# Two layers of cached attention and an MLP, decoded on one core: V rows placed by K chunk, and the softmax joins asked for an item later

## The chip, the cores and the metric

The kernel runs on one core of a Trainium2 chip. The core has five engines that run side by side, each with its own queue of instructions in a fixed order: TensorE (PE in the profile; PEld is its weight loading), VectorE (DVE), ScalarE (ACT), GpSimd (POOL) and SyncE (SP). Here SP only issues DMA transfers. The transfers are carried out by 16 DMA engines, which move data from the memory of the chip to the core's on-chip memory of 128 partitions. The metric is device microseconds for one execution. The kernel before takes 1147.62 us, the median of three runs from 1143.37 to 1153.54.

## The reference

Two blocks, A and B, are applied in turn, twice each. B's mixing part works on a sequence of one token, so that its shifted slices are all zero; what is left of it is a layer norm and an MLP. A is attention of one new token per row of the batch over a cache of keys and values. The batch has 8 rows; there are 16 query heads and 8 cache heads, 4096 cached positions and a head size of 256; the model width is 448.

```python
def _A_ref(x, k_cache, v_cache, wq, wo):
    q = (x @ wq).reshape(B, Sq, Hq, Dh)          # 8 x 1 x 16 x 256
    k = jnp.repeat(k_cache, rep, axis=1)         # two query heads share one cache head
    v = jnp.repeat(v_cache, rep, axis=1)
    scores = einsum(q, k) * (Dh ** -0.5)
    p = softmax(scores)
    return einsum(p, v).reshape(B, Sq, Hq * Dh) @ wo

x = A_x
x = x + _A_ref(_layernorm(x), A_k_cache, A_v_cache, A_wq, A_wo)
x = x + _B_ref(_layernorm(x), B_w1, B_w2, B_w3, B_w4)
x = x + _A_ref(_layernorm(x), A_k_cache, A_v_cache, A_wq, A_wo)
x = x + _B_ref(_layernorm(x), B_w1, B_w2, B_w3, B_w4)
```

Each pass over the attention reads both caches, 134 MB each, less what the kernel keeps on the chip from the first pass.

## The kernel before, in words

**Units, chunks, items.** One unit is one row of the batch and one pair of cache heads (`gp`, four pairs), in one of the two passes (`ps`). A unit's keys are cut into four chunks of 1 MB and its values too. An item is one chunk of K (`kv` 0), one chunk of V (`kv` 1) or one block of weights (`kv` 2). The order of the items is planned in Python before anything is issued (`block`, `first_kept`, `weights`), and one long loop over `items` (L1335) emits the instructions of each. The engines then run what was emitted in that order; an instruction waits for the semaphores of what it needs, and what stands behind it in its queue waits with it.

**Reads.** `emit_loads` (L972) walks the same list of items ahead of the work. It takes a free place of 8 KB on each partition (17 places, `places`) for each chunk and issues the read on SP: K by `load_k` (L949), V by `load_v` (L958; whole chunks at L967, halves at L970), weights by `load_weights` (L1017) and `load_tail` (L1011). SP stops at a read whose place is still in use. In `load_k` partition p takes consecutive rows of K from a region of 32 KB of its own. In `load_v` partition p takes 16 consecutive rows of V, 8 KB, and the 128 partitions of one chunk follow each other in memory.

**K items.** The chunk is transposed in blocks by VectorE (`transpose_k`, L1036); TensorE forms the scores of two chunks in `sc` (`scores`, L1051). After every second chunk the list `exps_due` is given an entry, and `flush` at the next item calls `exps` (L1059): VectorE takes the maximum over each partition's scores (as the minimum of the negated scores, L1061) and ScalarE writes the exponentials to `p_n` (L1062). A maximum is thus known for each partition and each half `u` of the chunks. With the second half comes the join: TensorE brings the two halves' maxima to all partitions (L1073, two matmuls of float32), ScalarE and VectorE choose between them with the mask `which` (even or odd pairs of partitions hold one half or the other, L1080 and L1087), VectorE finds the least (L1081) and subtracts it (L1091), and ScalarE takes the exponential (L1094). The result, `down`, corrects each partition's p to a common maximum.

**V items.** `turn_p` transposes p by TensorE (L1135) and VectorE scales it with `down` (L1142). `sum_p` sums p over the positions by TensorE (L549), and VectorE reduces and inverts the sums (L553, L559). `spread_p` copies p into the layout that the V products need (L1329), and `pv` multiplies p by V (L1154). All these small results share one bank, `misc`, so the next matmul into it has to wait until the last one was read.

**Between items** `step` advances generators that carry the rest of the layer: normalisation of the outputs (`half`, L589), the output projection, the MLP (`mlp`, with w3 by `wblk` at L503 and w4 at L463) and the next pass's query projection. Some of the V chunks stay on the chip for the second pass; `away` (L1116) and `back` (L1121) move parts of them.

Of the kernel before, what the change touches and what calls it, by code (L numbers as in the profile page):

```python
# [17 lines left out]
def kernel(  # L18
# [36 lines left out]
    assert D == 448 and F % 256 == 0  # L55
# [55 lines left out]
    def small(n):  # L111
# [5 lines left out]
    which = small(2)  # L117
    nc.vector.tensor_reduce(
        which,
        ident.rearrange("p (i u x) -> p u i x", u=2, x=2),  # L120
        mybir.AxisListType.XY,
        ALU.add,
    )
# [130 lines left out]


# [241 lines left out]
    def mlp_hidden(b0, nb):  # L497
# [3 lines left out]
        for c in range(HC):  # L501
            for fc in range(4):
                w, xi = wblk(w3_sb, F, c, fc)  # L503
                if nb == 1:
                    wide(h_ps[:, c : c + 1], w, xbs(1)[:, xi, :], fc == 0, fc == 3)
                    continue
                nc.tensor.matmul(
                    h_ps[:, c * nb : c * nb + nb],
                    w,
                    xbs(nb)[:, xi, :],  # L510
                    start=(fc == 0),
                    stop=(fc == 3),
                )
# [31 lines left out]
    def sum_p(who, p_of_unit):  # L545

        z_ps = misc[:, 0:32]
        for t in range(4):
# [3 lines left out]
        rz_of[who] = rz_free.pop(0)  # L552
        nc.vector.tensor_reduce(  # L553
            rz_t[:, rz_of[who]],
            z_ps.rearrange("p (n m) -> p n m", n=4),
            mybir.AxisListType.X,
            ALU.add,
        )
        nc.vector.reciprocal(rz_t[:, rz_of[who]], rz_t[:, rz_of[who]])  # L559
# [29 lines left out]
    def half(rec, ps, b, gps, OT, ready, tight=False):  # L589
# [8 lines left out]
        for k, gp in enumerate(gps):  # L598
            while (ps, b, gp) not in rz_of:
                yield  # L600
# [138 lines left out]
    q_rows = {4: (0, 0, 4), 5: (1, 0, 5), 7: (0, 4, 7)}  # L739
    q_final = [(1, 5, 8), (0, 7, 8)]  # L740
# [92 lines left out]
    for gp in free:  # L833
        weights("q", (gp, 0, Bn))
# [123 lines left out]
    def load_v(it, dst):  # L958
# [3 lines left out]
        src = rows.rearrange("(a p y) d -> a p (y d)", a=4, y=16)[it[2]]  # L962
        if halfway(it):
            nc.sync.dma_start(dst[:, 0 : PR * Dh], src[:, 0 : PR * Dh])
            nc.sync.dma_start(rest_t[:], src[:, PR * Dh :])
        elif loads and it not in halved:
            nc.sync.dma_start(dst, src)  # L967
        else:
            for y0, y1 in ((0, 8), (8, 16)) if loads else ((0, 8), (8, 12), (12, 16)):
                nc.sync.dma_start(dst[:, Dh * y0 : Dh * y1], src[:, Dh * y0 : Dh * y1])  # L970

    def emit_loads(most=None):  # L972
        n = 0
        while loads and places and n != most:
# [21 lines left out]
            if not open_:  # L996
                break
            p = pick(open_)
            taken(it, p)
            n += 1  # L1000
            if kv == 2:
                load_weights(slots[p], tasks[k][2], tasks[k][1])
# [14 lines left out]
    def load_weights(dst, kind, rows):  # L1017

        if kind == "o":
# [5 lines left out]
        src = A_wq[:, HU * rows[0] : HU * rows[0] + HU]  # L1025
        nc.sync.dma_start(
            dst[:, 0 : 3 * HU].rearrange("p (f c) -> p f c", f=3),
            src[0:384].rearrange("(f p) c -> p f c", f=3),
        )
        load_tail(dst[:, 3 * HU : 3 * HU + HU // 2], src)  # L1030
# [28 lines left out]
    def exps(p_sb, u):  # L1059
# [3 lines left out]
            p_sb[:, :, :, 2 * u : 2 * u + 2].rearrange("p t i x -> p x t i"),  # L1063
# [5 lines left out]
        if u == 0:  # L1069
            return  # L1070
        both = misc[:, 0:64]
        for k in range(2):
            nc.tensor.matmul(  # L1073
                both[:, 32 * k : 32 * k + 32],
                low_max[:, k : k + 1].to_broadcast([128, 128]),
                lanes[:],
                start=True,
                stop=True,
            )
        nc.scalar.mul(down, both[:, 0:32], which[:, 0:1])  # L1080
        nc.vector.tensor_reduce(  # L1081
            least,
            both.rearrange("p (u n m) -> p n u m", u=2, n=4),
            mybir.AxisListType.XY,
            ALU.min,
        )
        nc.vector.scalar_tensor_tensor(  # L1087
            down, both[:, 32:64], which[:, 1:2], down, ALU.mult, ALU.add
        )
        by_head = down.rearrange("p (n m) -> p n m", n=4)  # L1090
        nc.vector.tensor_tensor(  # L1091
            by_head, by_head, least.unsqueeze(2).to_broadcast([128, 4, 8]), ALU.subtract
        )
        nc.scalar.activation(down, down, ACT.Exp, scale=-1.0)  # L1094

    exps_due = []

    def flush():
        while exps_due:
            exps(*exps_due.pop(0))  # L1100
# [30 lines left out]
    def transpose_p(p_sb, p_to):  # L1131

        pt_ps = misc[:, 0:128].rearrange("p (t m) -> p t m", t=4)
        for t in range(4):
            nc.tensor.matmul(  # L1135
                pt_ps[:, t],
                p_sb[:, t].rearrange("p i x -> p (i x)"),
# [4 lines left out]
        nc.vector.tensor_tensor(  # L1142
            p_to, pt_ps, down.unsqueeze(1).to_broadcast([128, 4, 32]), ALU.mult
# [48 lines left out]
    emit_loads(2)  # L1192
# [28 lines left out]
    nc.sync.dma_start(w4_sb[:], B_w4.rearrange("(c p) d -> p c d", p=128))  # L1221
# [98 lines left out]
    def turn_p():  # L1320
        n = next(iter(p_of))
        slot_of[n] = free_slots.pop(0)
        transpose_p(p_of.pop(n), psv[slot_of[n]])

    def spread_p(it):
        if it in ring_of or it in plain or it[0] not in slot_of:
            return
        ring_of[it] = v_items.index(it) % 2
# [4 lines left out]
    kept_q = items[12]  # L1333

    for idx, it in enumerate(items):  # L1335
# [26 lines left out]
        if kv:  # L1362
            flush()
        if kv == 2:
# [8 lines left out]
            else:  # L1373
                gp_q, r0, r1 = rows
                nb = r1 - r0

                def q_of_block(c, fc, qw=slot):
                    if fc < 3:
                        return qw[:, fc * HU + 128 * c : fc * HU + 128 * c + 128], fc
                    k = 2 * 128 * c // HU  # L1380
                    at = 3 * HU + 128 * c - k * HU // 2
                    return qw[:, at : at + 128], 3 + k

                ps_q = (
                    store[0][:, 256 : 256 + 8 * nb] if nb == Bn else misc[:, 192 : 192 + 8 * nb]
                )
# [316 lines left out]
```

## Time and profile before

| what | value |
|---|---|
| median of the three runs | 1147.62 us |
| the profiled execution, its own time | 1153.23 us |
| its span from first to last instruction | 1151.1 us |
| mean granted clock of TensorE | 0.591 |
| TensorE busy | 732.3 us (64%) |
| weight loads busy | 472.2 us (41%) |
| VectorE busy | 654.0 us (57%) |
| ScalarE busy | 263.8 us (23%) |
| bytes read | 419.63 MB, 365 GB/s over the span |

The span is the profiled execution from its first instruction to its last; 2.1 us of the execution lie outside it. The chain that ended last is followed back from the last instruction to what released it, again and again; its shares tell what the time was spent waiting for. The costliest lines by busy time are the K transposes on VectorE (L1036, 445.7 us in 384 instructions), the scores on TensorE (L1051, 246.0 us) and the V products (L1154, 239.1 us). ScalarE's exponentials (L1062) take 105.9 us in 128 instructions, and the float32 matmuls of the joins (L1073) 74.2 us.

### The profile page before, as it was taken

To read this page: it belongs to the slowest core of one execution; us is meant where nothing else is said; L and a number is where in the kernel's file an instruction comes from. 1 tells how busy PE (TensorE), PEld (TensorE's weight loads), DVE (VectorE), ACT (ScalarE), POOL (GpSimd) and SP (SyncE) were. 2 spreads that over 40 slices of the span, in tenths; PEclk is the share of its full clock that TensorE was granted. 3 is DMA by queue.
4 is the path that set the end of the run, shared out by engine and by line. 5 is a ranking of instruction groups with operands and counts; after the bars stand their busy time and mean duration, and the time that the engine had idled before them with its cause. 6 is when DMAs were issued, how large, how long until landed. Compare 5 with 4: busy or idle time off the path is not lost.

```text
span 1151.1 us, 29813 instructions
## 1 busy us (share of the span) xinstructions
PE 732.3 (64%) x13109; PEld 472.2 (41%) x13109; DVE 654.0 (57%) x1388; ACT 263.8 (23%) x808; POOL 16.3 (1%) x27
## 2 busy tenths in 40 slices
PE   3255557665676667666775677557665775567776
PEld 2133334443354344433442345334433543345455
DVE  6255684188417851686258724782388237842764
ACT  1021111231124111422132114211421142112311
POOL 0000000000000000000000000000000000000000
PEclk9955555665655555556656575556655665575555
DMA  9999999988899779889989799987988998969994
GB/s 381 393 422 422 420 422 358 418 368 327 329 414 423 305 263 408 363 329 341 392 336 424 296 371 420 395 311 293 408 355 326 369 418 356 416 247 415 378 424 192
DMA packets 69297, 421.57 MB, mean 366 GB/s; under 512 B 7080, under 2 KB 12976, under 8 KB 43568
## 3 DMA queue, kind: packets, MB, share of 16 engines
q1 hardware_dynamic: 69120, 419.66, 90.8%
q8 instruction: 103, 1.69, 0.6%
q14 instruction: 26, 0.21, 0.0%
q10 hardware_dynamic: 48, 0.01, 0.0%
HBM read 419.63 MB, written 0.01 MB: 365 GB/s over the span
## 4 chain that ended last, share of the span: by engine, by line
DVE 36%; PE 27%; DMA 24%; ACT 6%; issue 4%; SPq 2%; POOL 0%; DVEq 0%; ACTq 0%
DVE places L1036 26%; DMA places<-in_A_v_cache_dram 16%; PE sc L1051 12%; DMA places<-in_A_k_cache_dram 9%; PE o L1154 6%; ACT p_n L1062 4%; DVE few L1061 3%; PE misc L210 2%; PE misc L625 2%; DVE store L1116 2%; DVE few L1081 1%; ACT down L1080 1%; SPq L967 1%; SPq L229 1%; DVE down L1087 1%
## 5 line engine op out<-in xcount | busy, mean ns | idle before, releaser
L1036 DVE STREAM_TRANSPOSE places<-places 128x512 uint32<-128x512 uint32 (+2 forms) x384 | 445.7, 1212 | 17.8 <-DMA places<-in_A_k_cache_dram 15.0
L1051 PE MATMUL sc<-places,qbd 128*8 128x256 bf16 (+1 forms) x4736 | 246.0, 362 | 191.3 <-DVE places L1036 174.3
L1154 PE MATMUL o<-places,ptw 128*8 128x256 bf16 x3808 | 239.1, 386 | 113.4 <-DMA places<-in_A_v_cache_dram 83.9
L1051 PEld LDWEIGHTS <-qbd 128*8 128x8 bf16 x4736 | 128.0, 106 | 263.8 <-issue 111.7
L1062 ACT ACTIVATE p_n<-sc,few 128x256 bf16<-128x256 f32 x128 | 105.9, 827 | 498.4 <-DVE few L1061 409.2
L1154 PEld LDWEIGHTS <-ptw 128*8 128x8 bf16 x3968 | 101.3, 104 | 174.7 <-issue 93.6
L1061 DVE TENSOR_REDUCE few<-sc 128x1 f32<-128x256 f32 x128 | 53.0, 414 | 96.2 <-PE sc L1051 80.1
L1073 PE MATMUL misc<-lanes,few 128*128 128x32 f32 x256 | 74.2, 393 | 30.4 <-DVE few L1061 17.1
L1329 ACT COPY ptw<-psv 128x32 bf16<-128x32 bf16 x248 | 54.0, 233 | 160.2 <-PE o L1154 151.3
L1073 PEld LDWEIGHTS misc<-lanes,few 128*128 128x128 f32 x256 | 59.3, 296 | 56.6 <-DVE few L1061 24.6
L625 PE MATMUL misc<-R_t,o_t 128*128 128x4 f32 (+1 forms) x212 | 48.7, 336 | 23.5 <-DVE R_t L601 9.6
L625 PEld LDWEIGHTS misc<-R_t,o_t 128*128 128x128 f32 x212 | 44.3, 290 | 40.5 <-ACT o_t L580 16.4
L1081 DVE TENSOR_REDUCE few<-misc 128x4 f32<-128x64 f32 x64 | 14.3, 224 | 71.6 <-ACT down L1080 71.6
L448 ACT CAST qbd<-misc 32x16 bf16<-32x16 f32 (+1 forms) x184 | 31.1, 169 | 53.9 <-PE misc L442 35.8
L1121 ACT COPY places<-store 128x1024 bf16<-128x1024 bf16 x40 | 39.4, 1029 | 2.9 <-PE o L1154 2.9
L629 DVE CAST qT<-misc 128x8 bf16<-128x8 f32 (+1 forms) x37 | 7.1, 191 | 57.2 <-PE misc L625 33.9
L553 DVE TENSOR_REDUCE rz<-misc 128x4 f32<-128x32 f32 x64 | 12.1, 189 | 42.2 <-PE misc L549 42.2
L210 PEld LDWEIGHTS <-w_sb 128*128 128x128 bf16 x896 | 28.1, 103 | 18.8 <-issue 18.1
L1142 DVE TENSOR_TENSOR psv<-misc,down 128x128 bf16<-128x128 f32 x64 | 18.3, 286 | 30.4 <-PE misc L1135 27.9
L580 ACT COPY o_t<-o 128x256 f32<-128x256 f32 x53 | 20.5, 388 | 53.6 <-PE o L1154 53.6
L549 PE MATMUL misc<-psv,few 128*128 128x32 bf16 x256 | 17.9, 190 | 23.5 <-DVE down L1087 16.9
L549 PEld LDWEIGHTS <-few 128*128 128x128 bf16 x256 | 13.1, 106 | 34.7 <-DVE down L1087 19.6
(166 smaller groups left out, 474.1 us busy)
## 6 DMA issues: line engine op xcount, KB each, us to landing
places<-in_A_k_cache_dram SPq DMA_DIRECT2D x79, 2048.0 KB, 12.4
places<-in_A_v_cache_dram SPq DMA_DIRECT2D x193, 512.0 KB, 7.3
places<-in_A_v_cache_dram SPq DMA_DIRECT2D x87, 1024.0 KB, 14.5
places<-in_A_k_cache_dram SPq DMA_DIRECT2D x34, 1024.0 KB, 11.3
places<-in_A_wq_dram SPq DMA_DIRECT2D x7, 768.0 KB, 9.7
rest<-in_A_v_cache_dram SPq DMA_DIRECT2D x8, 640.0 KB, 11.0
places<-in_A_v_cache_dram SPq DMA_DIRECT2D x8, 384.0 KB, 13.4
wo_sb<-in_A_wo_dram SPq DMA_DIRECT2D x1, 2688.0 KB
```

The lines of the kernel that those rows point to most:

```text
L210: nc.tensor.matmul(bass.AP(out.tensor, out.offset, [out.ap[0], (1, WIDE)]), w, x.to_broadcast([128, WIDE]), start=start, stop=stop, skip_g ...
L448: nc.scalar.copy(qbd[32 * a : 32 * a + 32, :, g0 : g0 + ng, a, :], qs.rearrange("p e (f g u h) -> p (e f) u g h", f=2, u=2, h=2)[:, :, u],)
L549: nc.tensor.matmul(z_ps, oneb.to_broadcast([128, 128]), p_of_unit[:, t], start=(t == 0), stop=(t == 3))
L625: nc.tensor.matmul(ot_ps[:, j], o_sb[:].rearrange("p (i j) -> p j i", j=2)[:, j], R, start=True, stop=True)
L1036: nc.vector.transpose(w, w)
L1051: nc.tensor.matmul(sc[32 * k : 32 * k + 8, 128 * (x % 2) : 128 * (x % 2 + nx)], qbd[:, ep, gp % 2].rearrange("p a h -> p (a h)"), v, start ...
L1061: nc.vector.tensor_reduce(low_max[:, u : u + 1], sc[:, 0:256], mybir.AxisListType.X, ALU.min)
L1062: nc.scalar.activation(p_sb[:, :, :, 2 * u : 2 * u + 2].rearrange("p t i x -> p x t i"), sc[:, 0:256].rearrange("p (x t i) -> p x t i", x= ...
L1073: nc.tensor.matmul(both[:, 32 * k : 32 * k + 32], low_max[:, k : k + 1].to_broadcast([128, 128]), lanes[:], start=True, stop=True,)
L1121: nc.scalar.copy(words, kept_words.bitcast(BF16))
L1154: nc.tensor.matmul(o_ps[32 * q : 32 * q + 8, :], ptz[:, at : at + 8], v[:, y * Dh : (y + 1) * Dh] if v2 is None or y < PR else v2[:, (y - ...
L1329: nc.scalar.copy(ptw[:, ring_of[it], :, 6:8].rearrange("p (t k) h -> p t k h", t=4), p_of_chunk(psv[slot_of[it[0]]], it[2]))
```

## The change

- V: the 128 pieces of 8 KB of one chunk go to other partitions. Piece number 4 i + c (i from 0 to 31, c from 0 to 3) goes to partition 32 c + i instead of 4 i + c. Partition blocks of 32 then belong to one chunk of K each, so the first 64 partitions of the turned p hold the first half of the chunks and the other 64 the second.
- Join: TensorE brings each half's maxima to the half of the partitions that needs it, with four matmuls of 64 columns; the mask `which` and the two instructions with it are left out. The write of p changes its order to suit.
- `exps_due` becomes `due_ops`, a list of pieces of work with the item at which they were asked for. Maxima with exponentials, the rest of a join (`join`), the scaling of p (`turn`) and the inverted sums (`total`) are put in it; `catch_up` carries out those that were asked for at an earlier item, and `free_misc` those that must be done before `misc` is written again.
- wq: the first two blocks become one item that takes two adjacent places and is read at once.
- w3 and w4: rows of w4 are read in pairs, and w3's columns are taken every second one to match.

```diff
-    which = small(2)
...
+    def w3blk(c, fc):
+        at = fc * F + 128 * c if fc < 3 else 3 * F + 128 * (c % 7)
+        xi = fc if fc < 3 else 4 - c // 7
+        if c % 7 == 6:
+            return w3_sb[:, at : at + 128], xi
+        at -= 127 * (c % 7 % 2)
+        return w3_sb[:, at : at + 255 : 2], xi
...
     def sum_p(who, p_of_unit):
+        free_misc()
         z_ps = misc[:, 0:32]
...
-        rz_of[who] = rz_free.pop(0)
-        nc.vector.tensor_reduce(
-            rz_t[:, rz_of[who]],
...
-        nc.vector.reciprocal(rz_t[:, rz_of[who]], rz_t[:, rz_of[who]])
+        def total():
+            k = rz_free.pop(0)
+            nc.vector.tensor_reduce(
+                rz_t[:, k],
...
+            nc.vector.reciprocal(rz_t[:, k], rz_t[:, k])
+            rz_of[who] = k
+        later("total", None, total)
...
+            tries = 0
             while (ps, b, gp) not in rz_of:
-                yield
+                if tries < 4:
+                    yield
+                elif due_ops:
+                    due_ops.pop(0)[3]()
+                tries += 1
...
-    for gp in free:
-        weights("q", (gp, 0, Bn))
+    weights("q2", q_first)
...
-        src = rows.rearrange("(a p y) d -> a p (y d)", a=4, y=16)[it[2]]
+        src = rows.rearrange("(a i c y) d -> a c i (y d)", a=4, i=32, c=4)[it[2]]
...
-        src = A_wq[:, HU * rows[0] : HU * rows[0] + HU]
+        at, n = (0, HF) if kind == "q2" else (HU * rows[0], HU)
+        src = A_wq[:, at : at + n]
...
+    due_ops = []
+    def later(kind, n, fn):
+        due_ops.append((now[0], kind, n, fn))
+    def catch_up(most=None):
+        while due_ops and due_ops[0][0] < (now[0] if most is None else most):
+            due_ops.pop(0)[3]()
+    def catch_up_all():
+        catch_up(len(items) + 1)
+    def free_misc():
+        while any(kind != "exp" for _, kind, _, _ in due_ops):
+            due_ops.pop(0)[3]()
...
-            p_sb[:, :, :, 2 * u : 2 * u + 2].rearrange("p t i x -> p x t i"),
+            p_sb[:, :, 2 * u : 2 * u + 2].rearrange("p t x i -> p x t i"),
...
+        free_misc()
         both = misc[:, 0:64]
         for k in range(2):
-            nc.tensor.matmul(
-                both[:, 32 * k : 32 * k + 32],
-                low_max[:, k : k + 1].to_broadcast([128, 128]),
-                lanes[:],
...
-        nc.scalar.mul(down, both[:, 0:32], which[:, 0:1])
-        nc.vector.tensor_reduce(
-            least,
...
-        nc.vector.scalar_tensor_tensor(
-            down, both[:, 32:64], which[:, 1:2], down, ALU.mult, ALU.add
-        )
...
+            for half_ in range(2):
+                nc.tensor.matmul(
+                    both[64 * half_ : 64 * half_ + 64, 32 * k : 32 * k + 32],
+                    low_max[:, (half_ + k) % 2 : (half_ + k) % 2 + 1].to_broadcast([128, 64]),
+                    lanes[:],
...
+        def join():
+            nc.vector.tensor_reduce(
+                least,
...
+            nc.vector.tensor_tensor(
+                down.rearrange("p (n m) -> p n m", n=4),
+                both[:, 0:32].rearrange("p (n m) -> p n m", n=4),
+                least.unsqueeze(2).to_broadcast([128, 4, 8]),
+                ALU.subtract,
+            )
+            nc.scalar.activation(down, down, ACT.Exp, scale=-1.0)
+        later("join", n, join)
...
-        nc.vector.tensor_tensor(
-            p_to, pt_ps, down.unsqueeze(1).to_broadcast([128, 4, 32]), ALU.mult
+        later(
+            "turn",
+            None,
+            lambda: nc.vector.tensor_tensor(
+                p_to, pt_ps, down.unsqueeze(1).to_broadcast([128, 4, 32]), ALU.mult
+            ),
         )
...
-    nc.sync.dma_start(w4_sb[:], B_w4.rearrange("(c p) d -> p c d", p=128))
+    w4_rows = B_w4.rearrange("(k x) d -> k x d", k=2)
+    w4_to = w4_sb[:].rearrange("p (k c) d -> p k c d", k=2)
+    for k in range(2):
+        nc.sync.dma_start(
+            w4_to[:, k, 0:6].rearrange("p (c j) d -> p c (j d)", j=2),
+            w4_rows[k, 0:768].rearrange("(c p j) d -> p c (j d)", p=128, j=2),
+        )
+    nc.sync.dma_start(w4_to[:, :, 6], w4_rows[:, 768:].rearrange("k p d -> p k d"))
...
         if kv:
-            flush()
+            catch_up()
...
-            flush()
+            if kept_now:
+                catch_up_all()
+            else:
+                catch_up()
```

## The prediction

> **What bounds the kernel now.** I read the page first: its slices, its queues and its chain.
>
> ```profile
> span 1151.1 us, 29813 instructions
> ...
> DMA  9999999988899779889989799987988998969994
> GB/s 381 393 422 422 420 422 358 418 368 327 329 414 423 305 263 408 363 329 341 392 336 424 296 371 420 395 311 293 408 355 326 369 418 356 416 247 415 378 424 192
> ...
> q1 hardware_dynamic: 69120, 419.66, 90.8%
> ...
> q10 hardware_dynamic: 48, 0.01, 0.0%
> ...
> DVE 36%; PE 27%; DMA 24%; ACT 6%; issue 4%; SPq 2%; POOL 0%; DVEq 0%; ACTq 0%
> ```
>
> The 16 DMA engines are busy for 90.8% of the span and reach 422 to 424 GB/s when nothing holds them back. The last chain nevertheless belongs to VectorE and TensorE for 63%: about every 119 us (eight times) there is a stretch bound by K transposes, scores and softmax, then one bound by V reads. At most 1151 - 419.66/0.422 = 157 us could be won by quicker compute. Anything that slows the reads has hardly any slack to hide in.
>
> So I read what the reads are, and how many engines they use.
>
> ```profile
> places<-in_A_k_cache_dram SPq DMA_DIRECT2D x79, 2048.0 KB, 12.4
> places<-in_A_v_cache_dram SPq DMA_DIRECT2D x193, 512.0 KB, 7.3
> places<-in_A_v_cache_dram SPq DMA_DIRECT2D x87, 1024.0 KB, 14.5
> places<-in_A_k_cache_dram SPq DMA_DIRECT2D x34, 1024.0 KB, 11.3
> ...
> out_dram<-places ACTq DMA_DIRECT2D x2, 1.8 KB
> places<-in_A_x_dram ACTq DMA_DIRECT2D x1, 7.0 KB
> ```
>
> Columns: number of reads, KB of one, us to landing. Queue q10 is ACT's: three transfers of 8 rows, 24 rows in all, and 48 packets. So each row is a packet and each transfer has 8 more, one closing packet for each engine that it ran on: 8 rows, 8 engines. On q1 the listed transfers (440) have 62,096 rows: K 113 x 128, V 298 x 128, weights 9,472, output 16. 69,120 - 62,096 = 7,024 closing packets = 438 x 16 + 2 x 8. Every read of 128 rows ran on all 16 engines, every transfer of 8 rows on 8. An engine moves 422/16 = 26.4 GB/s.
>
> **The V reads.** Before, a V chunk's source is 128 steps of 8 KB. In the changed program it is written as 4 steps (c, 8 KB apart), in each 32 (i, 32 KB apart), in each 8 KB: the outermost step counts 4, on a destination of 128 partitions. Bytes, rows and their size stay as they were. No transfer of the trace has an outermost step of 4, so the number of engines is bounded from both sides. By the total of rows it is 16, as for 128 rows; by the outermost step it is 4, as 8 was for 8. The nearest rows are the weight tails, whose source has two steps (64, in each 2) on 128 partitions:
>
> ```profile
> L1013 SPq DMA_DIRECT2D places<-in_A_wq_dram x8: 546/555/632, 1.3 to 1064.5; - x8
> ...
> L970 SPq DMA_DIRECT2D places<-in_A_v_cache_dram x195: 327/328/1247, 167.8 to 1122.7; - x195
> ```
>
> (ns of one issue, least, median and most). A source in two steps is issued in 555 ns instead of 328, so it is not simply flattened into 128 rows; its 16 closing packets fit either reading, as 64 is enough for 16. A queue that deals out by the outermost step, as the 8-row transfers look, gives V 4 engines. I take 4.
>
> [...]
>
> If it is 4, they are the same four each time, as no row shows a turn. V is 193 x 512 + 87 x 1024 + 8 x 640 + 8 x 384 + 2 x 256 = 196,608 KB = 201.3 MB; the rest is 419.66 - 201.3 = 218.3 MB, 4/16 of which, 54.6 MB, runs on those four too. Together 255.9 MB. Over the first DMA-bound windows (12 to 100 us, at 423, 409, 396 and 423 GB/s) the mean is 414 GB/s, 103.5 for four engines: 255.9/0.1035 = 2472 us. All compute of a period takes at most 119 us where the four engines now need about 300, so it hides. Added: 3 us at the start (312 GB/s in the first 12 us), 16 us from the last bytes (about 1135) to the end of the span, 2 us around it (1153.23 against 1151.1). Sum 2493 us; the median shown lies 0.5% below its profiled execution, but reads have no such margin, so I say 2490. At 424 GB/s it is 2414 + 21 = 2435. At 396 it is 2585 + 21 = 2606, and 32 more if the issue queue's eight long stands (L970 behind L1116, up to 16.1 us) each leave the four engines dry for 4: 2640.
>
> **The other parts matter only if V keeps 16 engines.** One join of before, from the timeline:
>
> ```profile
> 478.68 0.42 DVE L1061 TENSOR_REDUCE few<-sc 128x1 f32<-128x256 f32 x1 [0.56 <-PE sc L1051]
> 479.14 0.83 ACT L1062 ACTIVATE p_n<-sc,few 128x256 bf16<-128x256 f32 x1 [2.20 <-DVE few L1061]
> 479.15 0.50 PEld L1073 LDWEIGHTS misc<-lanes,few 128*128 128x128 f32 x2 [0.16 <-DVE few L1061]
> 479.83 0.29 ACT L1080 ACTIVATE down<-misc,few 128x32 f32<-128x32 f32 x1
> 480.15 0.23 DVE L1081 TENSOR_REDUCE few<-misc 128x4 f32<-128x64 f32 x1 [1.05 <-ACT down L1080]
> 480.29 0.24 DVE L1087 SCALAR_TENSOR_TENSOR down<-misc,few,down 128x32 f32<-128x32 f32 x1
> 480.57 0.19 DVE L1091 TENSOR_TENSOR down<-down,few 128x32 f32<-128x32 f32 x1
> ```
>
> VectorE stands still for 1.05 us between maximum and join, with the next transposes queued behind. The chain holds 53 such joins, 87.3 us with their exps, 1.65 each.
>
> - Asked an item later: in the changed program's order only 13 of 64 joins have transposes between maximum and join; 51 still follow their maximum directly. Maxima stand where they stood. 13 x (1.65 - 0.42 still done) = -16 us.
> - L1080 (287 ns) and L1087 (0.17 on the chain) go: VectorE's 0.17 x 40 = -7. L1080's place is taken by TensorE: before, one of two float32 matmuls comes after the second maximum (0.65 us to its end); now three of four half-wide ones do, 0.35 to 0.65 each, 1.05 to 1.95 where 1.05 was waited: 0 to +0.85 on 40 joins, 0 to +34. Behind them on TensorE stand sums and V products.
> - Sums (chain: L553 2.5, L559 2.1) and the scaling of p (L1142, 6.5, about half a wait) later: -8. They keep their place where scratch must be freed.
> - Exp now writes runs of 32 instead of every fourth element: between 826 ns as now and 388 (L580's copy of 256): -0.4 x the 12 chain pieces without a join = -5.
> - SP: 298 V issues of 0.555 us for 0.328 are +68 us of issuing, in a queue that mostly waits for places; about +5 reaches the path, at most 68.
> - wq's first halves: 768 rows of 2 KB (84 ns by the packet records) become 384 of 4 KB (159), 0.2 us of 16 engines; one pair of issues and one tail sort go, but the first projection waits for both halves: -1 to +1. w4's rows double, 5.2 to 4.5 us of 16 engines. w3's every-second-column weights cost what L1170's do, 103 ns, as L210's 103 now. POOL: nothing moves past it.
>
> Sum, without TensorE's term: -16 - 7 - 8 - 5 + 5 = -31.
>
> **Rivals.**
> - *V keeps 16 engines and the joins gain* (other side: faster). Place: the VectorE-bound stretches; price -31 + 0 to 20 for TensorE, from 1153: 1122 to 1142, less 0.5%: 1117 to 1135, 1125 in the middle. It decides as soon as one V read of 1 MB in an idle queue lands in about 3 us rather than 10. For it: K is read at 32 KB steps at full speed. Against it: the outermost 4. Chance 0.22.
> - *V keeps 16 engines and the join is no shorter*, as the 51 adjacent joins let it: 1153 - 31 + 34 = 1156, less 0.5%: 1150; the change then does not do what it says. Chance 0.11.
> - *V on 8 engines*: 201.3/8 + 218.3/16 = 38.8 MB an engine at 25.9 GB/s, 1498 + 21 = 1520. No row for it except that 8 was seen. Chance 0.04.
>
> **How the numbers follow.** Four engines have the remaining 0.63, so the time is 2490, its own range 2435 to 2640. Over all cases the range starts inside the first rival, at 1125 (half of its 0.22 is left out, and less than a tenth of the 0.63 above), and ends at 2640. A measurement of this kernel can tell about 1%, 11.5 us, from no change. Faster takes nearly all of the first rival, 0.21; within 1% is 0.09, from the second and the rim of the first; slower is 0.63 + 0.04 + the rest of the second, 0.70.
>
> **What would show it.** Four engines: the page's DMA row near 4 tenths (four full, twelve at 13.6 MB/25.9/2490 = 21%), 170 GB/s mean, V and K reads landing after 20 us and more, DMA most of the chain, and q1's packets. Rows become 62,096 - 384 - 128 - 768 = 60,816 and transfers stay 440 (two q reads and tails become one each, w4 three), so q1 has 60,816 + 7,024 = 67,840 packets on 16 engines and 298 x 12 fewer, 64,264, on 4. With 67,840 the forecast is wrong at its first step. Then L1081's successor shows the joins: VectorE's wait ahead of it above 1.05 us would mean the second rival, below it in 51 cases the first.

## The result, and the profile after

The changed kernel takes 2740.2 us (median of four runs, 2724.08 to 2746.29); the kernel before took 1150.58 us beside it. The ratio is 2.38, with a 95% interval from 2.365 to 2.398. The prediction's direction and its mechanism hold, but the time lies 250 us above the 2490 and 100 us above the upper end of 2640.

The page of the changed kernel, first the slices, the queues and the chain, then three groups of instructions (busy time and mean, then the idle time ahead of them and what ended it):

```profile
span 2721.9 us, 30190 instructions
...
DMA  9545642474246423752285227522752266226532
GB/s 278 156 142 169 179 146 106 149 226 136 105 139 219 147 104 117 236 162 106 111 253 135 105 105 240 180 105 105 228 162 123 106 236 176 106 105 222 158 122 89
...
q1 hardware_dynamic: 64264, 419.64, 46.8%
...
DMA 76%; SPq 8%; PE 6%; DVE 5%; another core or an unknown queue 4%; issue 1%; ACT 0%; DVEq 0%; ACTq 0%
...
L1196 PE MATMUL o<-places,ptw 128*8 128x256 bf16 x3808 | 261.9, 402 | 1615.0 <-DMA places<-in_A_v_cache_dram 1605.4
...
L1102 ACT ACTIVATE p_n<-sc,few 128x256 bf16<-128x256 f32 x128 | 60.6, 473 | 748.7 <-DVE few L1101 656.3
...
L1115 PE MATMUL misc<-lanes,few 128*64 128x32 f32 x512 | 62.5, 297 | 42.9 <-DVE few L1101 30.9
```

The packets are the prediction's number for four engines to the last one: 64,264. They lack 298 x 12 closing packets of the 67,840 that 16 engines would have left, so each of the 298 V reads ran on four engines. The bytes are those of before; the rate fell from 365 GB/s over the span to 154. The DMA row no longer stands near 9: it falls to 2 tenths at 104 to 106 GB/s, which is four of sixteen engines at full speed. TensorE's V products (L1196) wait 1605 us for V, against a chain that VectorE and TensorE led before. The two last rows show the rest of the change at work, hidden by those waits: an exponential takes 473 ns instead of 827, and the joins' matmuls are half as wide, 297 ns each instead of 393.

What the page doesn't tell is why 2472 us for the four engines were too few. The busy time in stretches of 12 us does (columns: the four compute engines and weight loads, the granted clock, the DMA share, GB/s):

```profile
core 0: us, PE busy (x) PEld busy (x) DVE busy (x) ACT busy (x) POOL busy (x), PEclk, DMA share, GB/s
...
1512.00:1524.00 12.00, 1.83 (x26) 0.76 (x26) 0.00 (x0) 0.45 (x2) 0.00 (x0) 0.50 0.25 106
1524.00:1536.00 12.00, 1.03 (x16) 0.51 (x16) 0.00 (x0) 0.22 (x1) 0.00 (x0) 0.50 0.25 106
...
1644.00:1656.00 12.00, 3.14 (x56) 1.79 (x51) 0.85 (x2) 1.15 (x6) 0.00 (x0) 0.50 0.71 198
1656.00:1668.00 12.00, 2.26 (x20) 1.75 (x21) 0.72 (x5) 0.79 (x3) 0.00 (x0) 0.50 0.97 239
1668.00:1680.00 12.00, 7.44 (x160) 6.64 (x160) 1.26 (x6) 2.28 (x8) 0.00 (x0) 0.50 0.79 293
```

Where V is read alone, a quarter of the engines is busy and moves 106 GB/s, a little more than the 103.5 that I had put in. Where K is read beside V, the engines are busy for 97% and move 239 GB/s: in the windows of before that the prediction used, nearly the same share (0.99) moved 423. The four engines are slower there too, and that is a loss that the sum doesn't have: rows of 4 KB, nearly all of them V's, take 160 ns on the average while five packets or fewer are in flight and 263 ns while 15 or more are, where they took 171 ns with 15 or more before. Counted over the packet records of the whole trace, exactly four packets are in flight for 1724 us, at 103 GB/s, and 15 or more for 735 us, at 282 GB/s. If the four engines are slowed in this proportion, they lose 735 x (1 - 282/414) = 234 us. With the prediction's 2472 us, 3 at the start and 16 at the end that gives 2725 us; the span is 2722.

### The profile page after: what moved, and what is told of

It reads as the page before. It is cut to its first block, busy times and chain, and to the rows that moved or that the text cites. A ratio compares the mean times of both kernels' runs of the same rounds, so it can differ in the third digit from the quotient of the medians.

```text
span 2721.9 us, 30190 instructions
## 1 busy us (share of the span) xinstructions
PE 767.9 (28%) x13364; PEld 480.8 (18%) x13364; DVE 644.0 (24%) x1321; ACT 212.5 (8%) x744; POOL 16.3 (1%) x27
## 3 DMA queue, kind: packets, MB, share of 16 engines
q1 hardware_dynamic: 64264, 419.64, 46.8%
## 4 chain that ended last, share of the span: by engine, by line
DMA 76%; SPq 8%; PE 6%; DVE 5%; another core or an unknown queue 4%; issue 1%; ACT 0%; DVEq 0%; ACTq 0%
DMA places<-in_A_v_cache_dram 72%; DMA places<-in_A_k_cache_dram 4%; DVE places L1060 3%; SPq L983 3%; PE sc L1075 3%; SPq L966 1%; PE o L1196 1%; DMA rest<-in_A_v_cache_dram 1%; SPq L978 1%; SPq L980 1%; PE misc L638 1%; PE misc L1115 1%; SPq L977 1%; DVE few L1101 0%
## 5 line engine op out<-in xcount | busy, mean ns | idle before, releaser
L1196 PE MATMUL o<-places,ptw 128*8 128x256 bf16 x3808 | 261.9, 402 | 1615.0 <-DMA places<-in_A_v_cache_dram 1605.4
L1196 PEld LDWEIGHTS <-ptw 128*8 128x8 bf16 x3968 | 108.0, 100 | 1703.1 <-issue 1648.7
L1075 PE MATMUL sc<-places,qbd 128*8 128x256 bf16 (+1 forms) x4736 | 255.3, 375 | 140.4 <-DVE places L1060 128.3
L1102 ACT ACTIVATE p_n<-sc,few 128x256 bf16<-128x256 f32 x128 | 60.6, 473 | 748.7 <-DVE few L1101 656.3
L1115 PE MATMUL misc<-lanes,few 128*64 128x32 f32 x512 | 62.5, 297 | 42.9 <-DVE few L1101 30.9
L1115 PEld LDWEIGHTS misc<-lanes,few 128*64 128x64 f32 x512 | 47.6, 206 | 69.6 <-DVE few L1101 37.3
L1154 DVE TENSOR_SCALAR store<-places 128x512 uint32<-128x512 uint32 x40 | 25.1, 681 | 11.2 <-DMA places<-in_A_v_cache_dram 11.0
```

The costliest lines, as they stand in the source:

```text
L1075: nc.tensor.matmul(sc[32 * k : 32 * k + 8, 128 * (x % 2) : 128 * (x % 2 + nx)], qbd[:, ep, gp % 2].rearrange("p a h -> p (a h)"), v, start ...
L1102: nc.scalar.activation(p_sb[:, :, 2 * u : 2 * u + 2].rearrange("p t x i -> p x t i"), sc[:, 0:256].rearrange("p (x t i) -> p x t i", x=2, ...
L1115: nc.tensor.matmul(both[64 * half_ : 64 * half_ + 64, 32 * k : 32 * k + 32], low_max[:, (half_ + k) % 2 : (half_ + k) % 2 + 1].to_broadcas ...
L1196: nc.tensor.matmul(o_ps[32 * q : 32 * q + 8, :], ptz[:, at : at + 8], v[:, y * Dh : (y + 1) * Dh] if v2 is None or y < PR else v2[:, (y - ...
```

## The experiments

Two things were to be told apart. The first is what the V read costs, and why it costs more than its engines. The second is what the rest of the change does when V is read on 16 engines. In all of them the kernel before took between 1149.6 and 1150.9 us beside them (medians).

### One part alone, and the number of engines

Only the V source is changed, as in the change (the destination, bytes and rows stay):

```diff
-        src = rows.rearrange("(a p y) d -> a p (y d)", a=4, y=16)[it[2]]
+        src = rows.rearrange("(a i c y) d -> a c i (y d)", a=4, i=32, c=4)[it[2]]
```

> The kernel before with the V source of the change and nothing else (V rows then meet the wrong p, so the output is not the reference's). If the four engines that an outermost step of 4 gives are the whole cause: the changed kernel's time again, 2740 us (2690 to 2790), and q1 with 69,120 - 298 x 12 = 65,544 packets. If the later joins and the rest add to the loss or make up for some: outside that, by up to 40 us.

Measured: 2754.23 us, ratio 2.394 (2.385 to 2.402), with 65,544 packets, 298 x 12 fewer than before. The read alone is the whole loss.

The same with 16 steps of 8 pieces, and with 8 steps of 16:

```diff
+        src = rows.rearrange("(a i c y) d -> a c i (y d)", a=4, i=8, c=16)[it[2]]
...
+        src = rows.rearrange("(a i c y) d -> a c i (y d)", a=4, i=16, c=8)[it[2]]
```

> The kernel before with V read in two steps whose outermost count is 16 (16 times 8 pieces of 8 KB, neighbours on partitions 128 KB apart in memory); V rows meet the wrong p. If only the outermost count decides: 16 engines, 69,120 packets on q1, the time of before within 1% (1140 to 1165 us), although each V issue takes 0.555 us as in the change. If reading V in pieces that lie apart is slow in itself, whatever the number of engines: 1500 us or more.

> The same with an outermost count of 8 (8 times 16 pieces); V rows meet the wrong p. Outermost count: 8 engines, 69,120 - 298 x 8 = 66,736 packets on q1, and by bytes 1520 us; with the same excess over the sum by bytes as the changed kernel has (2722 for 2491 in its span, 9%) 1660 us. If the count did not matter, the time of e2.

Measured: 1535.47 us with 16 steps, ratio 1.335 (1.328 to 1.342), and 1941.02 us with 8, ratio 1.687 (1.680 to 1.693). The packets, 69,120 and 66,736, are those of 16 and of 8 engines for each V read. So the number of engines does follow the outermost step: 4 steps ran on 4 engines (65,544 packets), 8 on 8 and 16 on 16.

The time, however, doesn't follow from the engines alone. The run with 16 steps missed the time of before and fell where I had put pieces that lie apart being slow in themselves, which the next section tests; the run with 8 steps fits none of its bands. In its packet records exactly eight packets are in flight for 903 us, at 177 GB/s or 22 per engine, where the four engines of the changed kernel moved 26 each: V alone slows eight engines, though not four. The page of the run with 16 steps, with landing times at its end:

```profile
span 1528.8 us, 29813 instructions
...
DMA  9999998999999999999999999999999989999995
GB/s 347 309 295 257 287 256 232 231 341 266 273 228 352 274 259 224 346 280 273 266 361 278 248 251 352 285 248 236 350 290 245 253 336 271 241 256 345 232 223 131
...
q1 hardware_dynamic: 69120, 419.66, 97.4%
...
places<-in_A_k_cache_dram SPq DMA_DIRECT2D x79, 2048.0 KB, 20.5
places<-in_A_v_cache_dram SPq DMA_DIRECT2D x193, 512.0 KB, 12.2
places<-in_A_v_cache_dram SPq DMA_DIRECT2D x87, 1024.0 KB, 32.0
```

All 16 engines are busy throughout, the packets are as many and as large as before, and yet they move 223 to 361 GB/s until the last slice: a V read of 1 MB lands after 32.0 us instead of 14.5, a K read of 2 MB, whose form is unchanged, after 20.5 instead of 12.4. In the packet records a row of 8 KB takes 512 ns on the average, 316 before. This second effect is what made the sum too small.

### What slows sixteen busy engines

Three things differ from before: the pieces of V lie at other addresses, the source has two steps, and a step covers fewer partitions (32, 16 or 8 instead of 128). First the addresses: the same steps, but each step reads one contiguous run of memory (256 KB with 4 steps, 64 KB with 16).

```diff
+        src = rows.rearrange("(c q i y) d -> q c i (y d)", c=4, q=4, i=32)[it[2]]
...
+        src = rows.rearrange("(c q i y) d -> q c i (y d)", c=16, q=4, i=8)[it[2]]
```

> The kernel before with V again in two steps of 4 and 32, but each of the four steps a run of 256 KB in one piece, 1 MB apart (V rows meet the wrong p). Four engines as in e1, the same partitions for each engine; only the memory addresses differ. Memory theory (engines that read neighbouring pieces of 8 KB at the same time slow each other and K): the excess goes, 2490 us as summed by bytes. On-chip theory (which partitions the engines write at the same time is what slows): e1's 2754 us.

> The same with 16 steps, each a run of 64 KB in one piece, 256 KB apart (V rows meet the wrong p): engines and partitions as in e2, other addresses. Memory theory: the time of before, 1140 to 1165 us. On-chip theory: e2's 1535 us.

Then the other way round, one step of 128 pieces that lie 32 KB apart:

```diff
+        src = rows.rearrange("(p q y) d -> q p (y d)", q=4, y=16)[it[2]]
```

> The kernel before with V in one step of 128 pieces of 8 KB that lie 32 KB apart, as K's chunks do (V rows meet the wrong p). Memory theory in its wide form (pieces that lie apart are slow) and any theory of the addresses alone: up to e2's 1535 us. If the two-step form (its engines and partitions) is what costs: the time of before, 1140 to 1165 us.

Measured: 2740.74 us (ratio 2.381, 2.369 to 2.394) and 1541.24 us (1.339, 1.333 to 1.345) with contiguous steps, 1141.01 us (0.991, 0.989 to 0.993) with one step. The times of the contiguous steps lie within 14 us of those of the scattered ones, and scattered pieces in one step are no slower than before. It isn't the memory addresses.

Last, sources of one step that write fewer partitions each: two reads of 64 partitions per chunk in the kernel before, and, in the changed kernel, four of 32 partitions with the same rows at the same places.

```diff
+            for h in range(2):
+                nc.sync.dma_start(to[64 * h : 64 * h + 64], src[64 * h : 64 * h + 64, e0:e1])
...
+            for c in range(4):
+                nc.sync.dma_start(to[32 * c : 32 * c + 32], src[c, :, e0:e1])
```

> The kernel before with each V read split into two transfers of 64 partitions, one step each, same rows on the same partitions; the sequence of addresses stays, 16 engines each. If what slows e2, e8 and e6 is the partitions that the engines write at the same time (not the two-step form, not the memory addresses): V's packets stretch here too, 1400 to 1550 us. If it is the two-step form: 1145 to 1175 us, the issues being twice as many.

> The changed kernel with its V layout, read as four transfers of 32 partitions for each chunk, so that the outermost count is 32. Outermost count and memory theory: 16 engines, near e4's 1110 us (up to 1160, because four times as many reads are issued, 0.33 us each or more). On-chip theory: 16 engines that write to 32 partitions at a time stay slow, 1300 to 1600 us.

Measured: 1571.71 us (ratio 1.365, 1.362 to 1.369) and 1532.0 us (1.330, 1.322 to 1.337). The queue line of the run with two halves:

```profile
q1 hardware_dynamic: 73888, 419.68, 96.6%
```

73,888 are 298 x 16 more than before: each half ran on 16 engines, from a source of one step, at the addresses and with the row sizes of before, and it is a little slower than the 16 steps (and than the 1550 us that I had put as its upper end). Neither the two-step form nor the addresses do it. What the slow runs on 16 engines have in common is that no step of a V read covers all 128 partitions: 64 in the run with two halves (1571.71 us), 32 with four reads (1532.0), 8 with 16 steps (1535.47 and 1541.24). The two with one step of 128, scattered or not, took 1141.01 and 1150.75 us. The run with two halves moves 267 GB/s over the span, with K's full-width reads among them, where 365 was had before. One row doesn't fit in: V alone on four engines, in steps of 32 partitions, ran at 106 GB/s, 26.5 per engine, without loss. The packet records of the run with 16 steps are uneven: 21% of the rows of 8 KB take the 309 ns (within 10%) that 98% of them take before, and 49% take 1.7 to 2.1 times as long. So that the partitions matter is shown, by exclusion of the rest; how they do is not, as the packet records name neither the engine nor the partition.

### The rest of the change, with V on 16 engines

The changed kernel with V read as before, and the same with only the maxima delayed (joins, scalings and sums are carried out at once):

```diff
-        src = rows.rearrange("(a i c y) d -> a c i (y d)", a=4, i=32, c=4)[it[2]]
+        src = rows.rearrange("(a p y) d -> a p (y d)", a=4, y=16)[it[2]]
...
     def later(kind, n, fn):
+        if kind != "exp":
+            return fn()
         due_ops.append((now[0], kind, n, fn))
```

> The changed kernel with V read as before; everything else of the change stays (rows of V and the joins' halves then don't belong together, so the output is not the reference's). First rival of the prediction, the joins gain: 1117 to 1135 us. Second rival, the join is no shorter: 1140 to 1160 us. If the rest of the change costs something of its own: above 1165.

> e4 with joins, scalings and sums carried out at once, as before; the shorter join and the closer write of p stay (V rows and the joins' halves don't belong together). The complement of e10: 1138 to 1155 us if the delay gains, 1105 to 1125 if the shorter join does. If each gives a part, the two gains should add up to e4's 41 us.

Measured: 1109.86 us (0.9636, 0.9611 to 0.9661), and 1110.4 us (0.9659, 0.9633 to 0.9685) without the delay. So the rest of the change is worth 41 us, and the delay nothing of it. Here is the row that the prediction named for the joins, from the first of the two runs:

```profile
L1124 DVE TENSOR_REDUCE few<-misc 128x4 f32<-128x64 f32 x64 | 13.9, 217 | 38.2 <-PE misc L1115 31.0
```

The opposite cut keeps the delay, wq, w3 and w4, and has the join of before with its mask and its write of p:

```diff
+        def join():
+            nc.scalar.mul(down, both[:, 0:32], which[:, 0:1])
+            nc.vector.tensor_reduce(
...
+            nc.scalar.activation(down, down, ACT.Exp, scale=-1.0)
+        later("join", n, join)
```

> The changed kernel with V read as before and with the longer join of before (mask, two matmuls of 128 columns, p written at every fourth element); what stays of the change is that joins, scalings and sums are asked for an item later, wq's first halves in one read, and w3/w4. If the delay is what gains in e4 (1110 against 1151): 1105 to 1125 us. If the shorter join and the closer write of p gain: 1138 to 1155 us. By the prediction's terms the delay is 24 of 31 us.

Measured: 1145.14 us (0.9946, 0.9923 to 0.9969): 6 us. Two parts were left for the 41, and each was done alone in the kernel before: the closer write of p, and the short join.

```diff
-            p_sb[:, :, :, 2 * u : 2 * u + 2].rearrange("p t i x -> p x t i"),
+            p_sb[:, :, 2 * u : 2 * u + 2].rearrange("p t x i -> p x t i"),
...
+            for half_ in range(2):
+                nc.tensor.matmul(
+                    both[64 * half_ : 64 * half_ + 64, 32 * k : 32 * k + 32],
...
-        nc.scalar.mul(down, both[:, 0:32], which[:, 0:1])
...
-        nc.vector.scalar_tensor_tensor(
-            down, both[:, 32:64], which[:, 1:2], down, ALU.mult, ALU.add
-        )
```

> The kernel before, where only the exponentials are written in runs of 32 elements (order x i) instead of every fourth; V is read as before, so rows of V and columns of p don't belong together in this run. Theory 'closer write' (most of the 41 us that remain of the change without its V read come from ScalarE's exponentials, 473 ns instead of 827, because joins and the next exponentials wait for ScalarE): 1112 to 1125 us. Theory 'shorter join' (the four half-wide matmuls and the dropped mask instructions give them): 1143 to 1150 us, that is 12 exponentials of the chain by 0.35 us, as my prediction's -5 us.

> The kernel before with only the short join: four matmuls of 64 columns and no mask; V is read and p written as before, so the maxima of the two halves are given to other partitions than they belong to. Theory 'closer write': 1140 to 1150 us. Theory 'shorter join': 1112 to 1125 us. The prediction's terms for this part alone (-7 for the mask, 0 to +34 for TensorE): 1144 to 1178 us.

Measured: 1143.9 us (0.9948, 0.9921 to 0.9975) with the closer write alone, 1115.33 us (0.9695, 0.9673 to 0.9718) with the short join alone. My favourite, the closer write, fell: it shortens each exponential from 827 to 474 ns and gives 6 us. The short join gives 34; the two gains add up to 40 of the 41. Its page, with the reduction that ends VectorE's wait (L1081 in both kernels); first the kernel before:

```profile
L1073 PE MATMUL misc<-lanes,few 128*128 128x32 f32 x256 | 74.2, 393 | 30.4 <-DVE few L1061 17.1
...
L1081 DVE TENSOR_REDUCE few<-misc 128x4 f32<-128x64 f32 x64 | 14.3, 224 | 71.6 <-ACT down L1080 71.6
```

Then the short join alone:

```profile
PE 712.8 (64%) x13365; PEld 455.6 (41%) x13365; DVE 644.4 (58%) x1324; ACT 252.0 (23%) x744; POOL 16.3 (1%) x27
...
L1074 PE MATMUL misc<-lanes,few 128*64 128x32 f32 x512 | 61.0, 290 | 38.1 <-DVE few L1061 26.1
...
L1081 DVE TENSOR_REDUCE few<-misc 128x4 f32<-128x64 f32 x64 | 14.4, 225 | 48.3 <-PE misc L1074 47.1
```

VectorE waits 48.3 us in 64 joins instead of 71.6, and is busy for 644.4 us instead of 654.0: 23.3 + 9.6 = 33 us, nearly the whole of the measured 34. What released the reduction was ScalarE's mask instruction; now it is TensorE. And TensorE is not late, as one join of this run shows on the timeline (start, duration):

```profile
483.52 0.39 DVE L1061 TENSOR_REDUCE few<-sc 128x1 f32<-128x256 f32 x1
...
483.96 0.50 PEld L1074 LDWEIGHTS misc<-lanes,few 128*64 128x64 f32 x6 [1.04 <-DVE few L1061]
483.96 0.63 PE L1074 MATMUL misc<-lanes,few 128*64 128x32 f32 x6 [0.91 <-DVE few L1061]
484.63 0.22 DVE L1081 TENSOR_REDUCE few<-misc 128x4 f32<-128x64 f32 x1 [0.73 <-PE misc L1074]
```

Three half-wide matmuls (x6, two records each) take 0.63 us together, no more than the 0.65 of the one full-width matmul that stood there before.

### Can it be had with V in one step?

With V in one step the partitions of the two halves alternate in pairs, so the mask is needed. Four versions keep p and V together. The first writes p pair by pair (two neighbours, then the next two) in the order of before; the second also spreads and masks the first maximum ahead of the second one.

```diff
-            p_sb[:, :, :, 2 * u : 2 * u + 2].rearrange("p t i x -> p x t i"),
-            sc[:, 0:256].rearrange("p (x t i) -> p x t i", x=2, t=4),
+            p_sb[:, :, :, 2 * u : 2 * u + 2],
+            sc[:, 0:256].rearrange("p (x t i) -> p t i x", x=2, t=4),
...
+        if u == 1:
+            spread_max(0)
+            nc.scalar.mul(down, both[:, 0:32], which[:, 0:1])
         nc.vector.tensor_reduce(low_max[:, u : u + 1], sc[:, 0:256], mybir.AxisListType.X, ALU.min)
```

> The kernel before, where ScalarE writes the exponentials pair by pair: the order of p in memory is the one of before, but two neighbours are written one behind the other instead of 256 times every fourth element. 'Closer write' with a price by distance: the exponential of 128x256 falls to 473 to 650 ns and the time to 1115 to 1140 us. If only the length of the runs counts (2 is no better than 1), the exponential stays at about 827 ns and the time at 1146 to 1152 us. 'Shorter join': 1143 to 1150 us in either case.

> The run with pairs, and the first half's maximum is spread by TensorE and multiplied by the mask on ScalarE ahead of the second maximum, so that the join no longer stands behind ScalarE's second exponential. If what costs is that the join waits for the second exponential on ScalarE (whatever the exponential's length), this gains 53 joins by 0.3 to 0.7 us beside the pairs' run: 1105 to 1125 us. If only the exponential's length counts, it is within 5 us of the pairs' run. If TensorE's instruction ahead of the scores delays them, it is up to 20 us slower than that run.

Measured: 1144.19 us (0.9947, 0.9928 to 0.9967) and 1146.06 us (0.9967, 0.9948 to 0.9986). Pairs are as good as runs of 32: 473 ns. The early mask gains nothing. Its groups show why:

```profile
L1064 PEld LDWEIGHTS misc<-lanes,few 128*128 128x128 f32 x256 | 60.4, 293 | 76.3 <-ACT down L1074 35.7
...
L1086 DVE TENSOR_REDUCE few<-misc 128x4 f32<-128x64 f32 x64 | 14.4, 225 | 70.9 <-PE misc L1064 70.9
```

TensorE's second matmul now waits for ScalarE's mask instruction (35.7 us), because both use the bank `misc`, and VectorE waits as long as before. This run moved the wait and so couldn't tell what the wait is worth.

So the mask's first half went to VectorE, in one instruction with the subtraction; then the pairs were added, then all the rest of the change.

```diff
-        nc.scalar.mul(down, both[:, 0:32], which[:, 0:1])
...
+        nc.vector.scalar_tensor_tensor(
+            down.rearrange("p (n m) -> p n m", n=4),
+            both[:, 0:32].rearrange("p (n m) -> p n m", n=4),
+            which[:, 0:1],
+            least.unsqueeze(2).to_broadcast([128, 4, 8]),
+            ALU.mult,
+            ALU.subtract,
+        )
```

> The kernel before, where the mask's first multiplication goes from ScalarE to VectorE and is put into one instruction with the subtraction; VectorE has as many instructions as before, TensorE the same matmuls, V is read as before. Theory 'ScalarE on the path' (the short join gains because VectorE no longer waits for ScalarE's mask instruction, which stands behind the second exponential): VectorE's idle time ahead of the join's reduction falls from 71.6 us to about 48 and the time by 17 to 24 us, to 1125 to 1133. Theory 'half-wide matmuls' (it gains because a matmul of 64 columns takes 290 ns and its weight load 198, against 388 and 291): 1146 to 1151 us.

> The same, and the exponentials are written pair by pair (473 ns for 827). If the pairs' 5 us came from ScalarE's mask instruction standing behind a shorter exponential, they are no longer to be had: within 3 us of the run with the mask alone. If they came from elsewhere, the two add: 1119 to 1129 us.

> The same with all of the change that is left when V is read as before: the joins, scalings and sums asked for an item later, wq's first halves in one read, w3 and w4. If the parts add, with the 6 us that they gave by themselves: 1113 to 1124 us. If the delay only hides the wait that the mask's move has already taken away: within 3 us of the run before it.

Measured: 1145.23 us (0.9958, 0.9934 to 0.9983), 1137.16 us (0.9894, 0.9858 to 0.993) and 1136.65 us (0.9896, 0.9865 to 0.9927). The first of them:

```profile
PE 728.8 (64%) x13109; PEld 470.7 (41%) x13109; DVE 664.2 (58%) x1388; ACT 252.1 (22%) x744; POOL 16.4 (1%) x27
...
L1080 DVE TENSOR_REDUCE few<-misc 128x4 f32<-128x64 f32 x64 | 14.4, 225 | 51.0 <-PE misc L1073 51.0
```

The wait falls by 20.6 us, nearly as with the short join, and with matmuls of full width: it was ScalarE's mask instruction that VectorE waited for, not the width of the matmuls. One join of each run says the same (above for the short join, here for the mask on VectorE): the reduction waits 0.73 us in both.

```profile
492.69 0.64 PE L1073 MATMUL misc<-lanes,few 128*128 128x32 f32 x2 [0.69 <-DVE few L1061]
493.37 0.23 DVE L1080 TENSOR_REDUCE few<-misc 128x4 f32<-128x64 f32 x1 [0.73 <-PE misc L1073]
```

But the time falls by 4.5 us only, near the band of the theory that the row speaks against. VectorE is busy for 10.2 us more than the 654.0 of before: on the timeline the join's three instructions of VectorE span 0.79 us (493.37 to 494.16) where they spanned 0.61 in the prediction's join (480.15 to 480.76). So of 20.6 us only 10.4 are left by its rows; why 6 of these don't reach the end stays open. The short join has both: the wait goes, and an instruction of VectorE with it. That this is what gains is read from the rows and not isolated. The last of the three runs and the changed kernel with V as before (1109.86 us) differ only in the mask, the width of these matmuls and the order in which p is written (474 ns per exponential in both); of the 27 us between them VectorE's rows give 23 (busy 661.5 us against 641.3, wait ahead of the join's reduction 41.4 against 38.2). No run drops the mask and keeps the matmuls at full width, so what their width gives besides is not known. The pairs add 8 us, with which that run fits neither of its bands, and the delay and the weights nothing more. The best version with p and V together is thus 13 us faster than the kernel before, a third of the 41.

## Why the prediction was right, and where it failed

**The V reads.** The step "I take 4" was right, by the packets and by the run with the V source alone. The number of engines followed the outermost step at 8 and 16 as well (66,736 and 69,120 packets). That they are the same four each time fits the 1724 us in which exactly four packets are in flight; no record names the engines.

**The time.** The failed step is the term "255.9/0.1035 = 2472 us". The bytes on the four engines were right, and so was 103.5 GB/s where V is read alone (103 to 106 measured). Wrong was to take that rate for the stretches with K as well, that is to assume that K and V side by side move 414 GB/s as before. They move 282, for 735 us, which costs the four engines 234 us by the packet records; the span exceeds 2472 + 19 by 231. The upper end of 2640 varied the rate only down to 396 GB/s and so couldn't hold it. The fault behind it was to treat a read as slow only by its number of engines, though the changed read also covers 32 partitions in a step instead of 128; with 16 engines, steps of 8 partitions cost 385 us (1535.47 against 1150.94).

**"All compute of a period ... hides."** Right: VectorE, TensorE and ScalarE together have 11% of the chain, and the changed kernel with the short join (2740) and the kernel before with only the V source (2754) differ by 14 us, a third of the 41 that they differ by when V is quick. Even these 14 may be no gain: the kernel before with V in four contiguous steps, which has the long join, took 2740.74.

**The other parts**, had V kept 16 engines: "-31 + 0 to 20 for TensorE" and "1117 to 1135" were too small a gain; it is 41 us, and 1110. The exponentials' -5 was right (-6). The delayed joins' -16 and the sums' -8 were wrong: delay and weights together gave 6 alone and nothing beside the short join. The joins' terms were mis-sized most: -7 for L1087 and 0 to +34 for TensorE stood where -34 was measured. I had priced each half-wide matmul at 0.35 to 0.65 us, where three take 0.63 together, and had taken L1080's 287 ns for replaced by them, while it was what VectorE stood still for.

**The rivals.** *V on 8 engines* was priced at 1520 us by the same sum by bytes; the run that made it so took 1941, with the same error in it, and eight engines are slower even where V is read alone (22 GB/s each, not 25.9). *The join no shorter* fell: VectorE's wait is 38.2 us in 64 joins in the changed kernel with V as before, 0.60 us each, below the 1.05 that the prediction named as the point.

**The checks.** Packets and chain came as announced; the landing times of V and K stand nowhere in the changed kernel's page. The DMA row swings between 2 tenths, where V is read alone, and 5 to 8, where K is read too; the 4 that was said is only about its mean. The mean rate, 155 GB/s where 170 was said, only restates the time. But the DMA share of q1, 46.8%, is higher than four full engines and twelve at 21% would make (41%): with the bytes unchanged, packets take longer, and this was the first sign on the page.

## What to carry to other kernels

Before a DMA's access pattern is changed, count its outermost step: here 4, 8 and 16 steps ran on 4, 8 and 16 engines, and the number of packets told it at once (12 fewer for each V read on four). Then ask whether the read still covers all 128 partitions in one step; where it doesn't, price it from a run. Here 16 engines, busy for 97.4% of the span, moved 274 GB/s with steps of 8 partitions, against 365 before, and the K reads beside them landed after 20.5 us instead of 12.4. And price a wait by what released it, here a small ScalarE instruction (287 ns), not by the big matmul beside it. Ask also who takes over the work of that instruction: with the mask on VectorE, 20.6 us less waiting made the kernel only 4.5 us faster.

## What the runs showed of the hardware

- With V read as two one-step reads of 64 partitions instead of one of 128 with the same rows, the kernel takes 37% longer (1571.71 against 1150.9 us), although the queue keeps 16 engines busy for 96.6% of the span.
- Four engines that read V alone move 26 GB/s each (103 in all, in steps of 32 partitions), eight move 22 each (177 in all, in steps of 16).
- K's reads are slower beside V reads that cover fewer than 128 partitions in a step, though they hadn't changed: K rows of 16 KB took 870 ns on the average in the changed kernel's packet records (steps of 32) and 777 with V read by halves (64), 631 before.
- ScalarE's 128x256 exponential takes 827 ns when it writes every fourth element, and 473 whether it writes pairs or runs of 32.
- Three float32 matmuls of 64 columns take 0.63 us in a row, about what one of 128 takes with its way in (0.65).
- With V read in 128 pieces of 8 KB that lie 32 KB apart the kernel is no slower than with a contiguous megabyte (1141.01 against 1150.75 us).
